# A six-layer cross network: moving small copies between engines and the fifth layer's remainder forward

## The chip, the cores and the metric

The kernel runs on one core of a Trainium2 chip. TensorE multiplies matrices into PSUM, ScalarE moves results from PSUM to SBUF and adds biases, VectorE does the elementwise arithmetic, GpSimd does small copies, and SyncE issues most of the DMAs. Each engine works through its own list of instructions in order and waits on semaphores for the others. The metric is the device time of the program in microseconds (us); lower is better. The median of the runs of the kernel before is 130.22 us (three runs, 130.12 to 130.40).

## The reference

The kernel computes a deep cross network with six layers for 4096 rows of 416 features, all in bfloat16:

```
x = x0
for l in range(6):
    x = x0 * (x @ ws[l] + bs[l]) + x
return x
```

`x0` is 4096x416, `ws` is 6x416x416, `bs` is 6x416. Every layer needs the whole previous `x`, but only of the same row.

## The kernel before, in words

The feature dimension of 416 is cut into three main chunks of 128 and a remainder of R = 32 features. In layers 0 to 4 the data is transposed: features lie on partitions, rows of the batch along the free dimension. `XM[i]` holds the three main chunks, `XR[i]` the remainder. The batch is cut into two halves s = 0 and 1 of 2048 rows; each half is four groups g of 512 columns. Because the remainder has 32 features only, its four groups are stacked on 4 x 32 partitions.

A tile (s, m) is the output chunk m of half s. `mm_full` (L206) multiplies the three main input chunks, `mm_row` (L212) adds the remainder's contribution, and `ew_main` evicts each half h of a tile: ScalarE adds the bias and writes bfloat16 (L170, in `ew_copy`), VectorE multiplies by x0 (L180) and adds the previous x (L181; L178 is layer 0's only step). Eviction uses four double banks of PSUM in rotation (`two_banks`).

The remainder's output is computed by `mm_rem` (L218 with the corner weights `WD`, L223 with the main chunks) and evicted by `ew_rem` (ScalarE L194; VectorE L197 in layer 0, L199 and L200 later). `rem_pair` does this for both halves of one layer; its matmuls read all the main chunks of the previous layer, both halves. `WD` holds a copy of the 32x32 corner of each layer's weights, at another place for each group, taken from `WR`, the last 32 weight rows (`fill_wd`, L134). `bsb` holds the biases for the last layer, copied onto four groups of 32 partitions (L111).

The order of work is written out by hand, and the program order is each engine's order. In layers 1 to 4 the six tiles go by pairs (ta, tb) for n = 0, 2, 4: full matmuls of ta, eviction of ta, for n = 2 the layer's remainder (`rem_pair`), full matmuls of tb, its row matmuls, the first row matmuls of the next tile, eviction of tb. The fifth layer (l = 4) is the one whose output feeds the last layer (`feeds_last`).

The last layer (l = 5) is computed the other way round: rows on partitions, 8 quads of four 128-row blocks, so that the output can be stored directly (`mm_q_full` L335, `mm_q_rows` L344 for the remainder and L348 for the bias from `bsb`). It needs the fifth layer's output in rows too, as `XLrows`: `xl_dmat` (L230) issues one DMA transpose for each tile when it is evicted. The remainder goes by a DMA transpose into a scratch tile `scrR` (L313) and by a copy into the last 32 columns of `XLrows` (L314). ScalarE casts (L403, for single blocks L416), VectorE multiplies by x0 (L404, L417) and adds `XLrows` (L405, L420), SyncE stores (L407, L409, L421).

At the start, `x0` arrives by eight DMA transposes on SyncE's queue (L77) and the remainder by three loads (L82, one on ScalarE's queue). `x0_rem` turns the remainder with VectorE transposes (L162) and copies (L163, L165). `first_layer(0)` and `first_layer(1)` do layer 0 for the two halves (L244, L252; evictions also by L187, L188 and L190 in `split_first`, and L271).

Of the kernel before, what the change touches and what calls it, by code (L numbers as in the profile page):

```python
# [16 lines left out]
def kernel(  # L17
# [7 lines left out]
    nc = tc.nc  # L25
    B, D = x0.shape
    L = ws.shape[0]
    P = 128
    NK = 3
    R = D - NK * P  # L30
    assert R == 32 and B == 4096 and D == 416 and L >= 2
    NS = 2
    NG = 4
# [20 lines left out]
    WR = const.tile([P, L, D], BF16)  # L54
    WD = const.tile([P, L, NG, R], BF16)
    bsb = const.tile([P, D], BF16)
# [4 lines left out]
    XLrows = big.tile([P, NBT, D], BF16)  # L61
    scrR = [big.tile([P, 4, P], BF16, name=f"scrR{s}") for s in range(NS)]
# [6 lines left out]
    def col0(s, g):  # L69
        return SW * s + CW * g  # L70
# [37 lines left out]
        nc.gpsimd.tensor_copy(bR[32 * g:32 * g + 32, :], bT[:, 4 * NK, 0:L])  # L108
    nc.gpsimd.tensor_scalar(out=bR[:, 0:1], in0=bR[:, 0:1], scalar1=1.0, scalar2=None, op0=ALU.add)
    for g in range(1, NG):  # L110
        nc.gpsimd.tensor_copy(bsb[32 * g:32 * g + 32, :], bsb[0:R, :])  # L111
    for g in range(1, NG):
        nc.vector.tensor_copy(WR[32 * g:32 * g + 32, 0, :], WR[0:32, 0, :])
        nc.scalar.copy(WR[32 * g:32 * g + 32, 1, :], WR[0:32, 1, :])
    load_x0t(0, 1)
# [13 lines left out]
    for q in range(8):  # L129
        nc.sync.dma_start(X0rows[:, 4 * q:4 * q + 4, :], x0_v[:, 4 * q:4 * q + 4, :])  # L130

    def fill_wd(l0, l1):
        for g in range(NG):
            nc.gpsimd.tensor_copy(WD[32 * g:32 * g + 32, l0:l1, g, :], WR[32 * g:32 * g + 32, l0:l1, NK * P:D])  # L134

    fill_wd(0, 1)

    PS = psum.tile([P, 8, CW], FP32)

# [3 lines left out]
    def two_banks():  # L143
        n = turn[0]
        i = first_order[n] if n < len(first_order) else (2, 1, 0, 3)[(n - len(first_order)) % 4]
        turn[0] += 1
        return PS[:, 2 * i:2 * i + 2, :]
# [10 lines left out]
    def x0_rem(s, p0, p1, parts):  # L158
        XRv = XR[0][p0:p1, CW * s:CW * s + CW].rearrange("p (j t) -> p j t", t=16)
        n = 16 // len(parts)  # L160
        for a, copy in enumerate(parts):
            nc.vector.transpose(out=xrt[s][p0:p1, n * a:n * a + n, :], in_=xrem[s][p0:p1, n * a:n * a + n, :])  # L162
            copy(XRv[:, :, n * a:n * a + n], xrt[s][p0:p1, n * a:n * a + n, :].rearrange("p t j -> p j t"))  # L163
        for a in range(p0, p1, 64):
            nc.vector.tensor_copy(XRx[s][64 - a:128 - a, :], XR[0][a:a + 64, CW * s:CW * s + CW])  # L165
# [71 lines left out]
    def first_layer(s):  # L237
        cur, nxt = XM[0], XM[1]

        def full(pt, m, h, gl, first, last):  # L240
            c0 = col0(s, 2 * h + gl)
            for k in range(NK):
                for q0, q1 in [(32 * q, 32 * q + 32) for q in range(4)] if s == 1 and h == 1 else ((0, P),):
                    nc.tensor.matmul(pt[q0:q1, gl, :], lhsT=WM[:, 0, k, 128 * m + q0:128 * m + q1], rhs=cur[:, k, c0:c0 + CW],  # L244
                                     start=(first and k == 0), stop=(last and k == NK - 1),
                                     tile_position=(0, q0) if s == 1 and h == 1 else None, skip_group_check=True)

        def row(pt, m, h, swapped, first):
            for gl in range(2):
                r0 = 32 * ((2 * h + gl + 2 * swapped) % 4)  # L250
                src = XRx[s][r0:r0 + 32, :] if swapped else XR[0][r0:r0 + 32, CW * s:CW * s + CW]
                nc.tensor.matmul(pt[:, gl, :], lhsT=WR[r0:r0 + 32, 0, 128 * m:128 * m + 128], rhs=src,  # L252
                                 start=first, stop=(not first), tile_position=(r0, 0), skip_group_check=True)

        pa = [two_banks() for m in range(NK)]
        for m, gl in ((0, 0), (1, 0), (2, 0), (0, 1), (1, 1), (2, 1)) if s == 0 else ((0, 0), (1, 0), (0, 1), (1, 1), (2, 0), (2, 1)):
            full(pa[m], m, 0, gl, True, False)
        pb = [two_banks()]
        row(pa[0], 0, 0, 0, False)
        if s == 1:  # L260
            row(pb[0], 0, 1, 0, True)
        row(pa[2], 2, 0, 0, False)
        row(pa[1], 1, 0, 1, False)
        if s == 0:
            closing = [split_first(s, 0, 0, pa[0], nxt)]
            closing.append(split_first(s, 2, 0, pa[2], nxt))
            t1 = ew_copy(0, 1, pa[1])
            for close in closing:
                close()
            x0_rem(0, 64, 128, (nc.scalar.copy, nc.vector.tensor_copy))  # L270
            nc.vector.tensor_tensor(out=nxt[:, 1, 0:2 * CW], in0=t1, in1=XM[0][:, 1, 0:2 * CW], op=ALU.mult)  # L271
            pb += [two_banks() for m in range(1, NK)]
            for m, gl in ((0, 0), (1, 0), (2, 0), (0, 1), (1, 1), (2, 1)):
                full(pb[m], m, 1, gl, True, False)
            row(pb[0], 0, 1, 0, False)
            row(pb[1], 1, 1, 0, False)
            row(pb[2], 2, 1, 1, False)
            split_first(s, 0, 1, pb[0], nxt)()
            x0_rem(1, 0, 128, (nc.vector.tensor_copy,))
            for m in range(1, NK):  # L280
                ew_main(0, s, m, 1, pb[m], cur, nxt)
            return None
        split_first(s, 0, 0, pa[0], nxt)()
        for m in (2, 1):
            ew_main(0, s, m, 0, pa[m], cur, nxt)
        full(pb[0], 0, 1, 0, False, False)
        rem_first(0)
        pb += [two_banks() for m in range(1, NK)]
        full(pb[1], 1, 1, 0, True, False)
        full(pb[0], 0, 1, 1, False, True)  # L290
        ew_main(0, s, 0, 1, pb[0], cur, nxt)
        full(pb[1], 1, 1, 1, True, False)
        for gl in range(2):
            full(pb[2], 2, 1, gl, True, False)
        row(pb[1], 1, 1, 0, False)
        row(pb[2], 2, 1, 1, False)
        pt = new_pts()
        mm_row(1, 0, 0, pt, XR[1], True, False)
        for m in range(1, NK):
            ew_main(0, s, m, 1, pb[m], cur, nxt)  # L300
        return pt
# [4 lines left out]
    def rem_pair(l, cur, curR, nxtR, feeds_last):  # L306
        pr2 = two_banks()
        for s in range(NS):
            mm_rem(l, s, pr2[:, s, :], cur, curR)
        for s in range(NS):  # L310
            ew_rem(l, s, pr2[:, s, :], curR, nxtR)
            if feeds_last:
                nc.sync.dma_start_transpose(out=scrR[s][:], in_=nxtR[:, CW * s:CW * s + CW])  # L313
                nc.gpsimd.tensor_copy(XLrows[:, 16 * s:16 * s + 16, NK * P:D].rearrange("p (g i) r -> p i g r", g=NG),  # L314
                                      scrR[s][:].rearrange("p i (g r) -> p i g r", g=NG))

    def rem_first(s):
        pr = two_banks()
        mm_rem(0, s, pr[:, 0, :], XM[0], XR[0])
        ew_rem(0, s, pr[:, 0, :], XR[0], XR[1])  # L320
# [29 lines left out]
                                 skip_group_check=True)  # L350

    first_layer(0)
    fill_wd(1, L)
    opened = first_layer(1)


    for l in range(1, LL):
        cur, curR = XM[1 + (l - 1) % 2], XR[1 + (l - 1) % 2]
        nxt, nxtR = XM[1 + l % 2], XR[1 + l % 2]
        feeds_last = (l == LL - 1)  # L360
        tiles = [(s, m) for s in range(NS) for m in range(NK)]
        pts = {tiles[0]: opened}

        def close(t):
            s, m = t
            for h in range(2):
                ew_main(l, s, m, h, pts[t][h], cur, nxt)
            if feeds_last:
                xl_dmat(s, m, nxt)

        for n in range(0, len(tiles), 2):
            ta, tb = tiles[n], tiles[n + 1]
            for g in range(NG):
                mm_full(l, ta[0], ta[1], g, pts[ta], cur, False, True)
            close(ta)
            if n == 0 and l == 1:
                rem_first(1)
            if n == 2:
                rem_pair(l, cur, curR, nxtR, feeds_last)
            pts[tb] = new_pts()  # L380
            for g in range(NG):
                mm_full(l, tb[0], tb[1], g, pts[tb], cur, True, False)
            mm_row(l, tb[0], tb[1], pts[tb], curR, False, True)
            opened = new_pts()
            if n + 2 < len(tiles):
                tc_ = tiles[n + 2]
                mm_row(l, tc_[0], tc_[1], opened, curR, True, False)
                pts[tc_] = opened
            elif not feeds_last:
                mm_row(l + 1, 0, 0, opened, nxtR, True, False)  # L390
            else:
                mm_q_rows((0,), (opened,), None)
            close(tb)

    o4 = [big.tile([P, NG, D], BF16, name=f"o4_{q}") for q in range(3)]

# [89 lines left out]
```

## Time and profile before

| what | value |
|---|---|
| median of the runs | 130.22 us |
| the profiled execution | 130.57 us, of which the span 128.8 us |
| TensorE busy | 122.7 us, 95% |
| VectorE busy | 105.2 us, 82% |
| ScalarE busy | 85.0 us, 66% |
| GpSimd busy | 9.2 us, 7% |
| granted TensorE clock | 0.999 |

The span runs from the first to the last instruction; some 1.8 us of the profiled execution lie around it. A line of the profile names the start and the length in us, the engine, the source line, the operation, the tile written and those read, the shapes, the number of instructions merged, and in brackets how long the engine was idle before and what ended that. A row with "q" behind the engine is a DMA issue on that engine's queue. A busy TensorE is not TensorE at its peak, since matmuls are pipelined and their ends are modelled.

### The profile page before, as it was taken

How to read it: one execution, taken by the hardware profiler on the slowest of the kernel's cores; microseconds unless marked ns; L12 is line 12 of the kernel's file. 1: busy time of each engine (PE TensorE's matmuls, PEld its weight loads, DVE VectorE, ACT ScalarE, POOL GpSimd, SP SyncE). 2: the span in 40 equal slices, each digit the busy share in tenths (PEclk: the TensorE clock that was granted, in tenths of full speed). 3: DMA queues.
4: the chain of work that ended last, by engine and by line, in shares of the span. 5: the costliest groups of instructions: out<-in, count | busy, mean ns of one | idle time of the engine just before them, and what ended most of it. 6: DMA issues, size and time to landing. Idle time of an engine off the chain costs nothing. (4 is left out here: it accounts for less than half of the span.)

```text
span 128.8 us, 4039 instructions
## 1 busy us (share of the span) xinstructions
PE 122.7 (95%) x1731; PEld 55.2 (43%) x1731; DVE 105.2 (82%) x192; ACT 85.0 (66%) x97; POOL 9.2 (7%) x29
## 2 busy tenths in 40 slices
PE   6999999999999999999999999999999999999960
PEld 3334344454454444444444544443444454554420
DVE  3347759648597989898989898989898999999991
ACT  2357558594976674966684966684966686676860
POOL 4282000040000000000000000000000050000000
PEclk9999999999999999999999999999999999999999
DMA  3999999999991000000000000000699989998563
GB/s 95 267 155 193 195 157 242 217 321 336 333 329 47 0 3 5 0 5 0 5 0 5 0 0 5 0 5 0 46 204 190 128 163 211 87 332 267 180 226 103
DMA packets 41933, 16.28 MB, mean 126 GB/s; under 512 B 30838, under 2 KB 41916, under 8 KB 41916
## 3 DMA queue, kind: packets, MB, share of 16 engines
q1 hardware_dynamic: 40384, 15.59, 56.4%
q10 hardware_dynamic: 1532, 0.44, 1.7%
q8 instruction: 13, 0.21, 0.7%
q14 instruction: 4, 0.03, 0.1%
HBM read 6.07 MB, written 3.41 MB: 74 GB/s over the span
## 5 line engine op out<-in xcount | busy, mean ns | idle before, releaser
L170 ACT ACTIVATE t<-PS,bM 128x1024 bf16<-128x1024 f32 x56 | 58.1, 1114 | 24.2 <-PE PS L212 22.8
L206 PE MATMUL PS<-XM,WM 128*32 128x512 bf16 x1152 | 65.2, 379 | 0.0
L206 PEld LDWEIGHTS <-WM 128*32 128x32 bf16 x1152 | 29.7, 97 | 33.8 <-issue 5.1
L180 DVE TENSOR_TENSOR t<-t,XM 128x1024 bf16<-128x1024 bf16 x48 | 33.3, 694 | 5.3 <-ACT t L170 5.3
L181 DVE TENSOR_TENSOR XM<-t,XM 128x1024 bf16<-128x1024 bf16 x48 | 33.7, 702 | 2.9
L335 PE MATMUL PS<-WM,XM 128*128 128x416 bf16 x96 | 17.9, 340 | 0.0
L244 PE MATMUL PS<-XM,WM 128*32 128x512 bf16 (+1 forms) x126 | 16.4, 379 | 0.2 <-DMA XM<-in_x_dram 0.2
L403 ACT CAST t<-PS 128x832 bf16<-128x832 f32 x12 | 10.1, 854 | 4.2 <-PE PS L335 3.1
L335 PEld LDWEIGHTS <-XM 128*128 128x128 bf16 x96 | 8.9, 98 | 8.6 <-issue 2.1
L244 PEld LDWEIGHTS <-WM 128*32 128x32 bf16 (+1 forms) x126 | 7.3, 97 | 8.6 <-issue 1.4
L223 PE MATMUL PS<-XM,WM 128*32 128x512 bf16 x120 | 8.2, 379 | 0.0
L405 DVE TENSOR_TENSOR o<-t,XLrows 128x832 bf16<-128x832 bf16 x12 | 7.1, 592 | 0.5
L212 PE MATMUL PS<-XR,WR 32*128 32x512 bf16 x96 | 7.5, 379 | 0.0
L314 POOL COPY XLrows<-scrR 128x512 bf16<-128x512 bf16 x2 | 1.6, 838 | 75.8 <-DMA scrR<-XR 75.8
L404 DVE TENSOR_TENSOR t<-t,X0rows 128x832 bf16<-128x832 bf16 x12 | 7.0, 585 | 0.0
L194 ACT ACTIVATE t<-PS,bR 128x512 bf16<-128x512 f32 x10 | 6.8, 696 | 0.0
L178 DVE TENSOR_TENSOR XM<-t,XM 128x1024 bf16<-128x1024 bf16 x7 | 4.7, 689 | 2.6 <-ACT t L170 2.5
L151 PE MATMUL PS<-warm 128*128 128x512 bf16 (+2 forms) x13 | 4.6, 536 | 1.0 <-DVE warm L87 1.0
L162 DVE STREAM_TRANSPOSE xrt<-xrem 64x256 bf16<-64x256 bf16 (+1 forms) x5 | 2.2, 476 | 4.0 <-DMA xrem<-in_x_dram 4.0
L187 ACT ACTIVATE t<-PS,bM 128x512 bf16<-128x512 f32 x4 | 2.6, 685 | 3.5 <-PE PS L252 3.5
L416 ACT CAST t<-PS 128x416 bf16<-128x416 f32 x8 | 4.0, 505 | 1.0 <-PE PS L335 0.8
L223 PEld LDWEIGHTS <-WM 128*32 128x32 bf16 x120 | 3.3, 97 | 3.2
(45 smaller groups left out, 55.6 us busy)
## 6 DMA issues: line engine op xcount, KB each, us to landing
X0rows<-in_x_dram SPq DMA_DIRECT2D x8, 416.0 KB, 7.8
WM<-in_ws_dram SPq DMA_DIRECT2D x5, 312.0 KB, 6.0
out_dram<-o SPq DMA_DIRECT2D x3, 416.0 KB, 4.0
out_dram<-o SPq DMA_DIRECT2D x6, 208.0 KB, 2.1
out_dram<-o SPq DMA_DIRECT2D x8, 104.0 KB, 1.7
WR<-in_ws_dram SPq DMA_DIRECT2D x4, 104.0 KB, 5.7
WM<-in_ws_dram ACTq DMA_DIRECT2D x1, 312.0 KB, 3.3
XM<-in_x_dram SPq DMA_TRANSPOSE x8, 4.8
```

The costliest lines, as they stand in the source:

```text
L170: nc.scalar.activation(t[:], pt.rearrange("p a b -> p (a b)"), ACT.Identity, bias=bM[:, m, l:l + 1], scale=1.0)
L180: nc.vector.tensor_tensor(out=t, in0=t, in1=x0c, op=ALU.mult)
L181: nc.vector.tensor_tensor(out=nxt[:, m, c0:c0 + 2 * CW], in0=t, in1=cur[:, m, c0:c0 + 2 * CW], op=ALU.add)
L194: nc.scalar.activation(tr[:, 0:CW], pr, ACT.Identity, bias=bR[:, l:l + 1], scale=1.0)
L206: nc.tensor.matmul(pts[g // 2][32 * q:32 * q + 32, g % 2, :], lhsT=WM[:, l, k, 128 * m + 32 * q:128 * m + 32 * q + 32], rhs=cur[:, k, c0:c ...
L212: nc.tensor.matmul(pts[g // 2][:, g % 2, :], lhsT=WR[32 * g:32 * g + 32, l, 128 * m:128 * m + 128], rhs=curR[32 * g:32 * g + 32, CW * s:CW ...
L223: nc.tensor.matmul(pr[32 * g:32 * g + 32, :], lhsT=WM[:, l, k, NK * P:D], rhs=cur[:, k, c0:c0 + CW], start=False, stop=(k == NK - 1), tile ...
L244: nc.tensor.matmul(pt[q0:q1, gl, :], lhsT=WM[:, 0, k, 128 * m + q0:128 * m + q1], rhs=cur[:, k, c0:c0 + CW], start=(first and k == 0), sto ...
L335: nc.tensor.matmul(py[g // 2][:, g % 2, 0:D], lhsT=xL[:, k, q_cols(q, g)], rhs=WM[:, LL, k, :], start=(first and k == 0), stop=((not first ...
L403: nc.scalar.copy(tv, py[h][:, :, 0:D])
L404: nc.vector.tensor_tensor(out=tv, in0=tv, in1=X0rows[:, b0:b0 + 5:4, :], op=ALU.mult)
L405: nc.vector.tensor_tensor(out=o, in0=tv, in1=XLrows[:, b0:b0 + 5:4, :], op=ALU.add)
```

## The change

Four things move:

- GpSimd's three copies of `bsb` go from the beginning to behind GpSimd's filling of the corner weights of layers 1 to 5, between the first layer's two halves.
- The four copies that fill layer 0's corner weights go from GpSimd to VectorE, into the first layer's first half, behind the first group's closing multiplications and ahead of the second part of `x0_rem`.
- The two copies of the remainder into `XLrows` go from GpSimd to ScalarE, and from right behind each transpose to behind the eviction of tile (1,0).
- In the fifth layer `rem_pair` comes behind the first tile (0,0) instead of the third (0,2), with its matmuls, evictions and the two transposes into `scrR`.

```diff
     for g in range(1, NG):
-        nc.gpsimd.tensor_copy(bsb[32 * g:32 * g + 32, :], bsb[0:R, :])
-    for g in range(1, NG):
         nc.vector.tensor_copy(WR[32 * g:32 * g + 32, 0, :], WR[0:32, 0, :])
...
-    def fill_wd(l0, l1):
+    def fill_wd(eng, l0, l1):
         for g in range(NG):
-            nc.gpsimd.tensor_copy(WD[32 * g:32 * g + 32, l0:l1, g, :], WR[32 * g:32 * g + 32, l0:l1, NK * P:D])
-
-    fill_wd(0, 1)
+            eng.tensor_copy(WD[32 * g:32 * g + 32, l0:l1, g, :], WR[32 * g:32 * g + 32, l0:l1, NK * P:D])
...
             for close in closing:
                 close()
+            fill_wd(nc.vector, 0, 1)
             x0_rem(0, 64, 128, (nc.scalar.copy, nc.vector.tensor_copy))
...
                 nc.sync.dma_start_transpose(out=scrR[s][:], in_=nxtR[:, CW * s:CW * s + CW])
-                nc.gpsimd.tensor_copy(XLrows[:, 16 * s:16 * s + 16, NK * P:D].rearrange("p (g i) r -> p i g r", g=NG),
-                                      scrR[s][:].rearrange("p i (g r) -> p i g r", g=NG))
+
+
+    def xl_rem():
+        for s in range(NS):
+            nc.scalar.copy(XLrows[:, 16 * s:16 * s + 16, NK * P:D].rearrange("p (g i) r -> p i g r", g=NG),
+                           scrR[s][:].rearrange("p i (g r) -> p i g r", g=NG))
...
     first_layer(0)
-    fill_wd(1, L)
+    fill_wd(nc.gpsimd, 1, L)
+    for g in range(1, NG):
+        nc.gpsimd.tensor_copy(bsb[32 * g:32 * g + 32, :], bsb[0:R, :])
     opened = first_layer(1)
...
-            if n == 2:
+            if n == (0 if feeds_last else 2):
                 rem_pair(l, cur, curR, nxtR, feeds_last)
...
             close(tb)
+            if feeds_last and n == 2:
+                xl_rem()
```

## The prediction

> **What bounds the kernel now.** The profiled execution took 130.57 us, a span of 128.8 and 1.77 around it; the median of the runs shown is 130.22, 0.35 less. I work out a difference within the span and take it off the median. I read the busy shares first, then the waits, then the order of time at the start, around 88 us and at the end.
>
> ```profile
> PE 122.7 (95%) x1731; PEld 55.2 (43%) x1731; DVE 105.2 (82%) x192; ACT 85.0 (66%) x97; POOL 9.2 (7%) x29
> ```
>
> TensorE is busy 95% of the span. Its few real waits lie in the first 21 us:
>
> ```profile
> 9.81 0.61 PE L252 MATMUL PS<-XR,WR 32*128 32x512 bf16 x4
> 14.68 0.60 PE L252 MATMUL PS<-XR,WR 32*128 32x512 bf16 x4 [0.19 <-DVE XR L163]
> 20.33 0.83 PE L244 MATMUL PS<-XM,WM 128*32 128x512 bf16 x12 [0.20 <-DMA XM<-in_x_dram]
> ```
>
> The first stands 0.53 us behind the matmul before it, where such a step elsewhere takes 0.31: 0.22 us lost. The third waits for an input transpose. From 20.33 to about 124.3 TensorE has no wait that another engine ends. Behind it VectorE works without a gap that matters from 98.75 to its last addition, and the chain that ended last is VectorE's alone. GpSimd shows inside that stretch:
>
> ```profile
> 103.45 1.62 POOL L314 COPY XLrows<-scrR 128x512 bf16<-128x512 bf16 x2 [75.80 <-DMA scrR<-XR]
> ...
> 102.74 0.69 DVE L180 TENSOR_TENSOR t<-t,XM 128x1024 bf16<-128x1024 bf16 x1
> 103.46 1.15 DVE L181 TENSOR_TENSOR XM<-t,XM 128x1024 bf16<-128x1024 bf16 x1
> 104.58 1.03 DVE L180 TENSOR_TENSOR t<-t,XM 128x1024 bf16<-128x1024 bf16 x1
> 105.65 0.69 DVE L181 TENSOR_TENSOR XM<-t,XM 128x1024 bf16<-128x1024 bf16 x1
> ```
>
> While the two GpSimd copies run, two VectorE instructions take 1.15 and 1.03 us instead of 0.69.
>
> **The change, part by part.**
>
> *The remainder's columns by ScalarE.* GpSimd's two copies leave the tail. The two slowed instructions fall back to 0.69, but the second, of tile (1,2), can't start before ScalarE's eviction ends at 103.44 + 1.11 = 104.55. So VectorE would start L404 not at 107.59 but about 0.4 earlier (0.35 of the second instruction, 0.03 of waiting). The first L405 also pays: it starts 0.68 after its L404, where others take 0.62, and the one at 117.35 the same; 0.06 each, for a list of semaphores with GpSimd's in it at the first. I count the first as gained.
>
> What it adds: two ScalarE copies of 128x512 behind tile (1,0)'s evictions, ahead of those of (1,1).
>
> ```profile
> 97.60 4.13 ACT L170 ACTIVATE t<-PS,bM 128x1024 bf16<-128x1024 f32 x4 [2.21 <-PE PS L212]
> 103.44 2.12 ACT L170 ACTIVATE t<-PS,bM 128x1024 bf16<-128x1024 f32 x2 [1.71 <-PE PS L212]
> 122.74 2.09 ACT L416 CAST t<-PS 128x416 bf16<-128x416 f32 x4 [0.59 <-PE PS L335]
> ```
>
> Queued behind them are two evictions, then a pause of 1.71 us. The price of one copy is not in the trace. The nearest low end is L416 and L114, ScalarE over 416 elements a partition in 0.51 and 0.54 us; L403 takes 0.85 for 832, so 0.83 ns an element, and 512 make 0.59 to 0.62. The high end is ScalarE's L163, 0.62 us for 256 elements read 64 bytes apart: doubled, 1.24. I take 0.61, since the new copy reads its rows in order and writes runs of 32 elements, and the same access pattern cost GpSimd 0.61 in the copy that VectorE did not hold up. ScalarE's neighbours in a row overlap by about 0.1 (4 of 1.11 in 4.13), so two copies are 1.0 to 1.25 us. Eviction (1,1) then starts at 99.6 + 1.0 to 1.25, ends at 101.7 to 102.0, and its second half at 102.7 to 103.0. VectorE, at 101.41 on that tile now, waits 0.3 to 0.6; two tiles at 1.33 a half bring it to (1,2) at 104.4 to 104.7, against the eviction at 104.55. It starts L404 between 107.2 and 107.4: still 0.2 to 0.35 early. TensorE wants those two banks for the rows of the last layer at 103.23 and finds them free by at least 0.2.
>
> [...]
>
> *How much of it reaches the end.*
>
> ```profile
> 117.91 0.85 ACT L403 CAST t<-PS 128x832 bf16<-128x832 f32 x1 [0.77 <-PE PS L335]
> 118.97 0.85 ACT L403 CAST t<-PS 128x832 bf16<-128x832 f32 x1 [0.20 <-PE PS L335]
> 118.99 0.58 DVE L404 TENSOR_TENSOR t<-t,X0rows 128x832 bf16<-128x832 bf16 x1
> 125.08 0.37 DVE L417 TENSOR_TENSOR t<-t,X0rows 128x416 bf16<-128x416 bf16 x1
> ```
>
> ScalarE's casts follow TensorE, which doesn't move. VectorE trails them by 1.3 us at L404's first and by less later: the cast that begins at 117.91 ends at 118.76 and VectorE takes it at 118.99. With 0.03 for the hand-over it can be earlier there by 0.19 at most. The last cast ends at 122.74 + 2.09 = 124.83, and its L417 starts at 125.08, so the end can come 0.21 earlier at most. A lead of 0.26 to 0.4 is therefore cut to 0.18: **gain 0.18 us**, and were the lead twice that, no more than 0.21.
>
> *The fifth layer's remainder behind tile (0,0)* (layer index 4). Its 32 matmuls, two evictions, four VectorE instructions and two transposes go past tiles (0,1) and (0,2), whose work comes 1.72 us later (L218 at 92.75 to the next L206 at 94.47). At (1,0) all is as before: VectorE has two idle stretches (0.29 at 91.18 and 0.22 at 98.75) that move about. The new wait: TensorE reads there the last tile of the layer before, whose last half VectorE writes at 87.41 + 0.69 = 88.10. Tile (0,0) starts at 84.31; now the remainder begins 2.60 behind such a start (90.15 to 92.75), and its matmuls on that half come 1.51 later (two groups into the second L223): 88.42. Slack 0.26 with the hand-over; cost 0. Without that cover every tenth late would be a tenth on TensorE, with all of its queue behind it.
>
> ```profile
> 87.41 0.69 DVE L181 TENSOR_TENSOR XM<-t,XM 128x1024 bf16<-128x1024 bf16 x1
> 90.92 2.90 SPq L230 DMA_TRANSPOSE XLrows<-XM  x1
> 98.77 3.75 SPq L313 DMA_TRANSPOSE scrR<-XR  x2
> ```
>
> On SP's queue the two L313 go past two L230: they are issued at about 93.9 and 95.8 and land 3.1 later by their row, so by 98.9, before ScalarE reaches its copy at 99.6 (GpSimd waited 4.6 from the first's issue to its start; that would be 100.4 for the second and 0.15 us of waiting). The L230 of (0,1) and (0,2) go from 97.6 and 99.4; with the longest landing of their row, 6.7, the data is there at 106.1, before L405 at about 108. Those of the second half are issued as now, when VectorE has written.
>
> *First corner weights by VectorE.* Four copies of 32x32 between L190, done at 12.39, and the transposes at 13.44: VectorE idles 1.05 there for a DMA. Bounds: 0.06 each by the smallest VectorE row (L93), 0.29 by L113 (32x416 with its step), so 0.24 to 1.16. Near the small end, I take 0.7 at most: cost 0. At 1.16 the wait at 14.68 would grow by 0.11, and the one at 20.33 would take that back.
>
> *GpSimd's bias copies later.* Three of 0.53 us leave 7.78 to 9.44. VectorE's L163 there took 0.49, its twin at 14.25 took 0.37, so the matmul at 9.81 can come 0.12 earlier. But the wait at 14.68 hangs on a DMA that lands at 13.42 and the one at 20.33 on one at 20.29, neither behind GpSimd: the 0.12 is swallowed, gain 0. The copies now run at about 27.7 to 29.4 beside L178 and L180; three of them can hold VectorE for 1.6 us, and it idles 0.31, 0.31 and 1.61 there up to 33.5; TensorE reads what L178 writes there from about 35 on. Cost 0. The copied rows are read first at 103.4.
>
> Sum: 0.18 + 0 + 0 + 0. 130.22 - 0.18 = **130.04 us** (the profiled kind of execution 130.39), a change of 0.14%. A measurement of this kernel can tell some 0.2%, 0.26 us, from no change, so this reads as none.
>
> **Rivals.**
>
> 1. *The input stream gives back more.* If the transposes behind 20.33 land 0.12 earlier than in this execution (their rows spread from 4.4 to 5.9), the early matmul's 0.12 stays, and TensorE's whole line comes forward: 0.12 + 0.18 = 0.30, 129.92 us. For it: both waits end on DMA. Against it: nothing in the change starts those DMAs sooner.
>
> 2. *ScalarE's copies are long and turn the pause into a queue.* At 1.24 each, 2.26 for the pair: (1,1)'s second half is evicted at 104.0 instead of 101.7, TensorE waits 0.8 at 103.23, VectorE starts L404 0.75 later; less what the first L405 saves, 130.22 + 0.65 = 130.87. It decides from about 0.75 a copy, where the banks come free too late and eat the 0.18. For it: L163. Against it: L114 and L416.
>
> 3. *The remainder waits for layer index 3.* If VectorE is 0.7 us later at 88.10 than now, TensorE stalls 0.44, and 130.22 + 0.44 - 0.18 = 130.48. Against it: the tiles there are tied to ScalarE's evictions, which wait for TensorE (1.7 us idle).
>
> 4. *The remainder's transposes land late.* The L230 of 96.89 landed 5.8 after its issue; so late, the second copy would start at 101.6, (1,1) be evicted by 104.2, TensorE wait 1.0: 131.0. For it: DMA engines are nearly full from 93 us. Against it: only one transpose stands ahead of these two.
>
> **How the numbers follow.** Forecast 0.46, its own range 129.96 to 130.3. Rival 1 with all that ends faster 0.30. Slower 0.24: rival 2 0.10, rival 3 0.06, rival 4 0.08. The range 129.8 to 130.6 takes rival 1 in, the forecast, rival 3 and half of rival 2's prices (0.9 to 1.0 a copy), and leaves some 0.2 out. Faster by over 0.2% 0.30, within 0.46, slower 0.24.
>
> **What the profile after would show.** L181's longest falls from 1.15 to 0.69 and no GpSimd row stands behind 30 us. ScalarE has two copies of 128x512 near 99.6, 0.6 each, and VectorE an idle of 0.3 to 0.6 before (1,1). L218 of the fifth layer starts near 86.9 without a wait before 88.4. TensorE's waits at 14.68 and 20.33 stand, the one at 9.81 is 0.12 shorter. L335 starts at 103.69 as now. VectorE's last addition comes 0.18 earlier, tied to the last cast by 0.03 to 0.1. Wrong would be a wait of TensorE at 88 or 103, a ScalarE copy above 0.75, or a first layer that ends earlier than now.

## The result and the profile after

The changed kernel takes 130.71 us (median of nine runs, 130.38 to 130.87) against 130.22 (nine runs, 129.89 to 130.48): a ratio of 1.0031, 95% interval 1.0017 to 1.0045. It is slower by 0.3%, where 0.14% faster was forecast. Later runs of the same two programs put the ratio at 1.0017 (1.0005 to 1.003), so the size is nearer 0.2%. The profiled execution after took 130.72 us, its span 128.9; the one before 130.57 and 128.8, which was slower than any of before's nine timed runs. That turned out to matter.

Nearly every step that was forecast is there. Here are rows picked from the timeline of the changed kernel (start and length in us); rows between them are left out, also where no "..." stands. Its line numbers differ by a few: L132 answers to L134, L166 to L170, L176 and L177 to L180 and L181, L208 to L212, L214 to L218, L240 to L244, L310 and L315 to L313 and L314, L336 to L335, L408 and L409 to L403 and L404, L422 and L425 to L417 and L420.

```profile
12.91 0.70 DVE L132 COPY WD<-WR 32x32 bf16<-32x32 bf16 x4
...
20.14 0.83 PE L240 MATMUL PS<-XM,WM 128*32 128x512 bf16 x12
...
86.87 0.39 PE L214 MATMUL PS<-XR,WD 128*32 128x512 bf16 x4
...
93.92 2.52 SPq L310 DMA_TRANSPOSE scrR<-XR  x2
...
99.56 1.14 ACT L315 COPY XLrows<-scrR 128x512 bf16<-128x512 bf16 x2
100.59 2.13 ACT L166 ACTIVATE t<-PS,bM 128x1024 bf16<-128x1024 f32 x2
101.75 0.69 DVE L176 TENSOR_TENSOR t<-t,XM 128x1024 bf16<-128x1024 bf16 x1 [0.30 <-ACT t L166]
103.64 3.34 PE L336 MATMUL PS<-WM,XM 128*128 128x416 bf16 x18
104.54 0.69 DVE L176 TENSOR_TENSOR t<-t,XM 128x1024 bf16<-128x1024 bf16 x1
107.20 0.58 DVE L409 TENSOR_TENSOR t<-t,X0rows 128x832 bf16<-128x832 bf16 x1
118.75 0.59 DVE L409 TENSOR_TENSOR t<-t,X0rows 128x832 bf16<-128x832 bf16 x1 [0.19 <-ACT t L408]
125.15 0.65 DVE L425 TENSOR_TENSOR o<-t,XLrows 128x416 bf16<-128x416 bf16 x2
```

No GpSimd row stands behind 30 us. The fifth layer's remainder begins at 86.87 without a wait. Its transposes are issued at 93.9, ahead of ScalarE's copies at 99.56, and these take 1.14 together (0.62 each). VectorE waits 0.30 for the eviction behind them. Its first multiplication of the last layer starts at 107.20 instead of 107.59, from 118.75 on it is tied to ScalarE's casts, and its last addition ends at 125.81 instead of 126.02: 0.21 earlier. TensorE's last layer starts at 103.64, 0.05 earlier than before. Up to VectorE's end the forecast gain is there.

It is lost behind that, in work that nobody touched. The last stores, of the kernel before (L421) and then of the one after (L426): the view of the tile `out_dram` from 124.6 us on, durations of the issue in ns, and the time from issue to landing:

```profile
L421 SPq DMA_DIRECT2D out_dram<-o x4: 332/332/369, 124.3 to 126.2; - x4
DMA to landing us min/median/max: 1.7/1.7/1.7
```

```profile
L426 SPq DMA_DIRECT2D out_dram<-o x3: 332/333/728, 125.0 to 126.0; - x3
DMA to landing us min/median/max: 2.1/2.2/2.4
```

The same stores of 104 KB land 0.4 to 0.7 later after their issue, and the last of them takes 0.728 us to issue instead of 0.369. The DMA queues between 124.5 and 126.9 us, before and then after (packets, MB, share of the 16 DMA engines):

```profile
q1 hardware_dynamic: 573, 0.43, 53.4%
```

```profile
q1 hardware_dynamic: 556, 0.41, 51.2%
q14 instruction: 1, 0.01, 1.9%
```

One packet on queue 14, of kind "instruction", is new among the stores. The trace gives it 8192 bytes and a start at 125.84 us; 1.9% of 16 engines over 2.4 us are 0.73 us on one engine. That it is a piece of an engine's program is the author's reading of that kind; which engine's list it moves with is measured below. Another packet of this size on this queue comes in every profile 0.1 to 0.4 us behind the last data of the stores (127.66 in before, 127.85 in after). It is not the one that moves, though the expectation for before again takes it for that one, and it is not counted below. The last store landed at 127.91 before and at 128.11 after: 0.21 earlier by VectorE, 0.41 later by its landing.

### The profile page after: what moved, and what is told of

It reads as the page before. It is cut to its first block, busy times and chain, and to the rows that moved or that the text cites. A ratio compares the mean times of both kernels' runs of the same rounds, so it can differ in the third digit from the quotient of the medians.

```text
span 128.9 us, 4033 instructions
## 1 busy us (share of the span) xinstructions
PE 123.1 (95%) x1730; PEld 55.0 (43%) x1731; DVE 105.3 (82%) x196; ACT 86.0 (67%) x99; POOL 7.2 (6%) x23
## 3 DMA queue, kind: packets, MB, share of 16 engines
HBM read 6.07 MB, written 3.41 MB: 74 GB/s over the span
## 4 chain that ended last, share of the span: by engine, by line
PE 87%; DVE 5%; DMA 4%; ACT 1%; issue 1%; DVEq 0%
PE PS L202 49%; PE PS L240 13%; PE PS L336 9%; PE PS L208 5%; PE PS L219 5%; DMA XM<-in_x_dram 4%; PE PS L214 2%; DVE o L425 2%; PE PS L248 2%; DVE t L422 1%; PE PS L345 1%; DVE o L410 1%; DVE t L409 1%; PE PS L349 1%; ACT t L408 1%
## 5 line engine op out<-in xcount | busy, mean ns | idle before, releaser
L166 ACT ACTIVATE t<-PS,bM 128x1024 bf16<-128x1024 f32 x56 | 58.2, 1114 | 22.9 <-PE PS L208 21.8
L176 DVE TENSOR_TENSOR t<-t,XM 128x1024 bf16<-128x1024 bf16 x48 | 32.9, 686 | 5.7 <-ACT t L166 5.7
L177 DVE TENSOR_TENSOR XM<-t,XM 128x1024 bf16<-128x1024 bf16 x48 | 33.4, 696 | 2.6
L336 PE MATMUL PS<-WM,XM 128*128 128x416 bf16 x96 | 17.9, 340 | 0.0
L240 PE MATMUL PS<-XM,WM 128*32 128x512 bf16 (+1 forms) x125 | 17.2, 386 | 0.1
L408 ACT CAST t<-PS 128x832 bf16<-128x832 f32 x12 | 10.1, 854 | 4.2 <-PE PS L336 2.7
L336 PEld LDWEIGHTS <-XM 128*128 128x128 bf16 x96 | 8.9, 98 | 8.6 <-issue 2.1
L240 PEld LDWEIGHTS <-WM 128*32 128x32 bf16 (+1 forms) x126 | 7.3, 99 | 9.5 <-issue 3.0
L208 PE MATMUL PS<-XR,WR 32*128 32x512 bf16 x96 | 7.5, 379 | 0.0
L409 DVE TENSOR_TENSOR t<-t,X0rows 128x832 bf16<-128x832 bf16 x12 | 7.0, 584 | 0.2 <-ACT t L408 0.2
L421 ACT CAST t<-PS 128x416 bf16<-128x416 f32 x8 | 4.0, 505 | 1.0 <-PE PS L336 0.8
L184 DVE SCALAR_TENSOR_TENSOR XM<-PS,bM,XM 128x512 bf16<-128x512 f32 x4 | 2.9, 746 | 1.2 <-PE PS L248 1.2
```

Source lines behind the costliest of these rows:

```text
L166: nc.scalar.activation(t[:], pt.rearrange("p a b -> p (a b)"), ACT.Identity, bias=bM[:, m, l:l + 1], scale=1.0)
L176: nc.vector.tensor_tensor(out=t, in0=t, in1=x0c, op=ALU.mult)
L177: nc.vector.tensor_tensor(out=nxt[:, m, c0:c0 + 2 * CW], in0=t, in1=cur[:, m, c0:c0 + 2 * CW], op=ALU.add)
L208: nc.tensor.matmul(pts[g // 2][:, g % 2, :], lhsT=WR[32 * g:32 * g + 32, l, 128 * m:128 * m + 128], rhs=curR[32 * g:32 * g + 32, CW * s:CW ...
L336: nc.tensor.matmul(py[g // 2][:, g % 2, 0:D], lhsT=xL[:, k, q_cols(q, g)], rhs=WM[:, LL, k, :], start=(first and k == 0), stop=((not first ...
L408: nc.scalar.copy(tv, py[h][:, :, 0:D])
```

## The experiments

Two questions were open: which half of the change costs the time, and whether the late stores are the cost or a sign of something else. The theory that formed from the traces: such a transfer follows a fixed entry of ScalarE's instruction list, and the two added copies move it from behind the end to among the last stores. Rivals: TensorE gets through layer 0 later ("front" in the expectations, where the theory of the transfer is called "end" and later "page"); the time comes from the earlier remainder or from ScalarE's copies themselves (with the earlier transposes, "ports" in the expectations); it is GpSimd's shorter list that moves the transfer; the stores meet `XLrows`' last transposes.

**Both kernels again, and each half alone.** The first two are the programs before and after, unchanged. The third has the tail part (remainder forward, copies by ScalarE) and the start as before; the fourth the start part (corner weights by VectorE, bias copies later) and the tail as before. Against the changed kernel, the edit of the third and of the fourth:

```diff
     for g in range(1, NG):
+        nc.gpsimd.tensor_copy(bsb[32 * g:32 * g + 32, :], bsb[0:R, :])
+    for g in range(1, NG):
...
+    fill_wd(nc.gpsimd, 0, 1)
...
-            fill_wd(nc.vector, 0, 1)
...
     fill_wd(nc.gpsimd, 1, L)
-    for g in range(1, NG):
-        nc.gpsimd.tensor_copy(bsb[32 * g:32 * g + 32, :], bsb[0:R, :])
```

```diff
-    def xl_rem():
-        for s in range(NS):
-            nc.scalar.copy(XLrows[:, 16 * s:16 * s + 16, NK * P:D].rearrange("p (g i) r -> p i g r", g=NG),
-                           scrR[s][:].rearrange("p i (g r) -> p i g r", g=NG))
+                nc.gpsimd.tensor_copy(XLrows[:, 16 * s:16 * s + 16, NK * P:D].rearrange("p (g i) r -> p i g r", g=NG),
+                                      scrR[s][:].rearrange("p i (g r) -> p i g r", g=NG))
...
-            if n == (0 if feeds_last else 2):
+            if n == 2:
...
-            if feeds_last and n == 2:
-                xl_rem()
```

> The kernel before, unchanged, as a control. In the two profiles so far VectorE's last addition ends at 126.02 before and 125.81 after, 0.21 earlier as forecast, yet the last store lands at 127.91 before and 128.11 after. Two theories for the loss of 0.49 us in the medians. 'End': an 8192-byte instruction transfer at 125.84, among the last stores of the kernel after, holds three of them up by 0.4 to 0.7 each; before, the transfer starts at 127.66, behind the last row of output. 'Front': TensorE gets through layer 0 later; the profiled execution of before (130.57) was slower than each of its nine timed runs (129.89 to 130.48), so its front may not be the usual one. Here both expect a ratio of 1.000 within 0.0015. End: no 8192-byte transfer between 124.5 and 127.0, last store 1.6 to 1.75 us from issue to landing. Front: the first matmul behind the last input transpose, at 20.33 in the first profile, comes 0.2 to 0.5 earlier in this one.

> The kernel after, unchanged, as a control. Both theories expect a ratio of 1.0031 within 0.0015. End: again an 8192-byte transfer within the last stores, between 125.5 and 126.2, and the last two stores at 2.1 us or more from issue to landing. Front: no such thing need be there; layer 0's last half starts 0.2 to 0.5 later than in the usual execution of before.

> The tail's two parts alone: the remainder's columns by ScalarE, the fifth layer's remainder behind tile (0,0); the beginning is as before. By the forecast's own sum 130.22 - 0.18 = 130.04, ratio 0.9986. End, if the tail's parts bring the transfer forward: VectorE's last addition 0.2 earlier than before but ratio 1.002 to 1.004. Front: the forecast's gain stays, ratio 0.998 to 0.9995, and VectorE's last addition near 125.8.

> The beginning's two parts alone: the corner weights' four copies by VectorE, GpSimd's bias copies behind layer 0's first half; the tail is as before, GpSimd's two copies in it too. Forecast: no change, ratio 1.000. Front: the whole loss and the missing gain are here, ratio 1.003 to 1.006. End: ratio 1.000 if the tail's parts move the transfer, 1.003 if these do (GpSimd's or VectorE's number of instructions).

Measured, with twelve runs each and 35 of the kernel before (130.26 us):

| run | us | ratio, 95% | queue-14 packet among the last stores | issue to landing of the last three stores |
|---|---|---|---|---|
| before again | 130.14 | 0.9992 (0.9978 to 1.0006) | none | 1.66, 1.67, 1.78 |
| after again | 130.52 | 1.0017 (1.0005 to 1.003) | 125.97, 0.69 us | 2.31, 2.15, 2.06 |
| tail part only | 130.56 | 1.002 (1.001 to 1.003) | 125.86, 0.76 us | 2.49, 2.25, 2.13 |
| start part only | 130.17 | 0.9992 (0.9979 to 1.0005) | none | 1.66, 1.67, 1.80 |

The loss is all in the tail part, and it comes with the packet. The start part is worth nothing that can be measured. The front theory had its sign in before again: the first matmul behind the last input transpose stands there at 19.75 us instead of 20.33. But that time moves from execution to execution in both kernels: over all twelve profiles of this document it is 19.75 to 20.33 with the old start (seven profiles, mean 20.09) and 19.86 to 20.33 with the new one (five, mean 20.03).

Before, run again, also showed what the forecast gain was worth: its last addition ended 1.02 us behind ScalarE's last cast, as in after, not 1.19 as in the execution that the prediction was made from. GpSimd's two copies stood elsewhere against VectorE. The timelines of this run:

```profile
102.70 1.69 POOL L314 COPY XLrows<-scrR 128x512 bf16<-128x512 bf16 x2 [76.72 <-DMA scrR<-XR]
```

```profile
102.22 0.68 DVE L180 TENSOR_TENSOR t<-t,XM 128x1024 bf16<-128x1024 bf16 x1
102.94 0.98 DVE L181 TENSOR_TENSOR XM<-t,XM 128x1024 bf16<-128x1024 bf16 x1
104.06 0.87 DVE L180 TENSOR_TENSOR t<-t,XM 128x1024 bf16<-128x1024 bf16 x1
106.90 0.58 DVE L404 TENSOR_TENSOR t<-t,X0rows 128x832 bf16<-128x832 bf16 x1
```

GpSimd starts 0.24 ahead of VectorE's L181 instead of 0.01, the two slowed instructions take 0.98 and 0.87 instead of 1.15 and 1.03, and the last layer begins early enough that the casts set the end.

**Is it ScalarE's list, whatever is in it?** Four kernels move the list alone. Counted with its waits, the trace of before has 192 entries on ScalarE, that of after 194. The first edit takes after back to 192, by giving two of ScalarE's weight copies at the start to VectorE. The second adds two copies of one column to before near 4 us, where ScalarE is idle. The third adds three small memsets to GpSimd in the kernel with the tail part only, so that its list is as long as before's (48 entries); the diff shows this against the tail part alone, without the line that allots `spare`. The fourth adds eighteen one-column copies to after, in ScalarE's pauses in layers 1 to 3; their results are used by nothing.

```diff
-        nc.scalar.copy(WR[32 * g:32 * g + 32, 1, :], WR[0:32, 1, :])
+        (nc.scalar.copy if g == 1 else nc.vector.tensor_copy)(WR[32 * g:32 * g + 32, 1, :], WR[0:32, 1, :])
```

```diff
     nc.scalar.activation(dz[:, 1:2], dz[:, 0:1], ACT.Identity, bias=dz[:, 0:1], scale=1.0)
+    for _ in range(2):
+        nc.scalar.copy(dz[:, 1:2], dz[:, 0:1])
```

```diff
     fill_wd(nc.gpsimd, 1, L)
+    for _ in range(3):
+        nc.gpsimd.memset(spare[:], 0.0)
```

```diff
             close(tb)
+            if n == 0 and not feeds_last:
+                for _ in range(6):
+                    nc.scalar.copy(dz[:, 1:2], dz[:, 0:1])
```

> The kernel after, with two of ScalarE's three early copies of layer 1's remainder weights given to VectorE, so that ScalarE's list is as long as before (two fewer than after). Theory 'page': the 8192-byte transfer is ScalarE's next piece of program; after's two added copies let ScalarE reach the end of a piece right at its last instruction (transfer 1.05 after its last cast in three profiles), before it reached it only behind the kernel. Then this one has no 8192-byte transfer between 124.5 and 126.8, stores that land in 1.65 to 1.8, and the forecast's gain: ratio 0.9986, 0.997 to 0.9995. Rival 'GpSimd': GpSimd's shorter list or its early end moves the transfer; then it stays near 125.9 and the ratio at 1.002 to 1.003. Rival 'ports': ScalarE's copies or the earlier transposes themselves slow the last stores; ratio 1.002 to 1.003 without the transfer.

> The kernel before, with two ScalarE copies of one column more, in its idle time near 4 us; nothing else is changed. Page: the transfer comes at 125.5 to 126.2, about 1.05 behind ScalarE's last cast, the last three stores land in 2.1 to 2.5 instead of 1.7, ratio 1.003 to 1.004 (the delay of 0.4 us without the tail's gain). GpSimd and ports: ratio 1.000, transfer near 127 to 127.7.

> The tail's parts alone, and three tiny GpSimd fills of a spare tile behind 27 us, so that GpSimd's list is as long as before. GpSimd: the transfer goes back behind 127, ratio 0.9986. Page and ports: nothing changes against the tail's parts alone, transfer at 125.8 to 126, ratio 1.002 within 0.0015.

> The kernel after, with 18 ScalarE copies of one column more, six in each of three idle stretches of ScalarE in layers 1 to 3. Page: ScalarE reaches the end of its piece 18 list entries earlier, some nine casts before its end, so the transfer comes at 118.5 to 120.5; the stores of that time are late, those of the end are not (1.65 to 1.8), ratio 0.9986, 0.997 to 1.000. GpSimd and ports: transfer at 125.9 or none, ratio 1.002 to 1.003.

Measured, with twelve runs each and 35 of the kernel before (130.24 us):

| run | us | ratio, 95% | queue-14 packet among the last stores | issue to landing of the last three stores |
|---|---|---|---|---|
| after, list as before | 130.14 | 0.9987 (0.9974 to 1.0001) | none | 1.65, 1.66, 1.79 |
| before, two more | 130.51 | 1.002 (1.0005 to 1.0034) | 125.78, 0.78 us | 2.47, 2.22, 2.09 |
| tail part, GpSimd's list as before | 130.46 | 1.0018 (1.0007 to 1.0028) | 125.63, 0.76 us | 2.49, 2.25, 2.11 |
| after, eighteen more | 130.07 | 0.9987 (0.9975 to 0.9999) | none (118.65, 0.31 us) | 1.66, 1.67, 1.82 |

The second is the decisive one: the kernel before, with two copies of a single column 100 us ahead of the end, gets all of the loss. Its ratio is below the 1.003 to 1.004 that was expected, but the interval still excludes no change. Its view of `out_dram` from 124.3 us, then its queues between 125.5 and 126.8, and last the view of `out_dram` of after with the list as before, whose queues have no instruction row in that stretch:

```profile
L423 SPq DMA_DIRECT2D out_dram<-o x4: 332/332/767, 124.1 to 125.9; - x4
DMA to landing us min/median/max: 1.7/2.2/2.5
```

```profile
q14 instruction: 1, 0.01, 3.7%
```

```profile
L426 SPq DMA_DIRECT2D out_dram<-o x3: 332/332/369, 124.8 to 125.8; - x3
DMA to landing us min/median/max: 1.7/1.7/1.8
```

GpSimd's list has nothing to do with it, and neither have the copies themselves, the remainder's place or the transposes: the kernel with eighteen more has all of the change, and its last stores land as fast as before's. Its packet comes at 118.65 and takes 0.31, 7 us ahead of the last store. There an expectation missed: the stores of that time were to be late, but those issued at 117.08, 118.21 and 119.61 land in 2.09, 2.07 and 2.04 us, and the same stores take 2.03 to 2.25 in the other profiles. The packet fell into a pause between the data of two stores. The busy share of the 16 DMA engines between 118 and 119.5 us, in 40 slices of 0.0375 us, is below a tenth from 118.68 to 119.09:

```profile
DMA  6899999999999987470000000000045999989998
```

**How sharp is the place?** One added copy, and six, in the same line as the two above, with one run of each beside one of before (130.58 us).

> The kernel before with one tiny ScalarE copy near 4 us instead of two: one look, for the edge. In the ten traces so far the 8192-byte transfer follows ScalarE's 191st list entry; with two more that entry is its last before the closing barrier, with one more it would be the barrier's first entry, behind the last store's landing. Page: no such transfer between 124.5 and 126.8, the last store in 1.7 to 1.85, TensorE's last matmul to the end of the span 4.65 to 4.85. If it is not one entry that decides, but ScalarE's early extra work, the transfer is at 125.5 to 126.2 and that stretch is 4.95 to 5.1.

> The same with six. Page: the 191st entry is four earlier than with two, two casts before ScalarE's end; the transfer comes at about 124.0 to 125.2, the stores issued from 123.5 to 124.5 are the late ones, the last one lands in 1.7 to 2.0, and from TensorE's last matmul to the end of the span it is 4.7 to 4.95, between the two cases.

One more took 130.74, six more 130.40. With one more no packet falls among the stores; it comes at 129.27, and the last stores land in 1.66, 1.66 and 1.75 us. With six more it comes at 124.18 and takes 0.59; two earlier stores, issued at 123.57 and 124.13, land in 2.21 and 1.98, and the last three in 1.66, 1.66 and 1.78, so the end pays nothing. In ordinary words, from the records of ScalarE's list (the entry's end, and the start of the 8192-byte packet behind it; a drain is the record's DRAIN, a wait its EVENT_SEMAPHORE, and the closing barrier is the group of these behind the last store):

```
kernel             entries   191st entry                      packet starts
before               192     drain of the closing barrier     128.33 -> 129.34
before, one more     193     wait of the closing barrier      128.26 -> 129.27
after                194     drain behind the last cast       124.83 -> 125.84
before, two more     194     drain behind the last cast       124.76 -> 125.78
before, six more     198     wait ahead of the last but one   123.20 -> 124.18
after, 18 more       212     wait among the pairs' casts      117.50 -> 118.65
```

In the profiles of before, after and all ten runs this packet follows the end of the 191st entry by 1.0 to 1.3 us, and where the entry moves it moves with it. In after, where the two copies stand behind it, an earlier such packet (46.74 us, behind the 63rd entry) keeps its place; in before with two more, where they stand ahead of it, it moves from 46.78 to 43.78. This earlier place is less sharp. Where the 63rd entry is a wait (seven profiles) the packet comes 1.01 to 1.03 behind its end, but where it is an activation (five) the packet comes before that activation has ended; in all twelve it comes 1.01 to 1.06 behind the start of the 62nd. So the distance of 128 entries between the two places is good to about one entry; 8192 bytes by 128 make 64 bytes an entry, an estimate from these two places alone. Among the last stores the packet's cost was not hidden: it is 0.30 us at the end of the span (worked out below).

Another expectation missed. With one more, the end of the span came 5.135 us behind the start of the last matmul, where 4.65 to 4.85 was expected, though its stores were fast. That is some 0.4 more than in the profiles without the packet among their stores (4.72, below). The larger part stands in its VectorE rows (the timelines of GpSimd and VectorE of that run):

```profile
103.34 1.72 POOL L316 COPY XLrows<-scrR 128x512 bf16<-128x512 bf16 x2 [77.23 <-DMA scrR<-XR]
```

```profile
103.34 0.69 DVE L183 TENSOR_TENSOR XM<-t,XM 128x1024 bf16<-128x1024 bf16 x1
104.46 1.14 DVE L182 TENSOR_TENSOR t<-t,XM 128x1024 bf16<-128x1024 bf16 x1 [0.43 <-ACT t L172]
```

Here GpSimd and VectorE started within 0.001 us of each other. VectorE took its 0.69, and GpSimd's first copy 1.16 instead of 0.61. VectorE then had to wait for the eviction and was held up itself, 1.14 for 0.69, on the instruction that nothing covers. The lag of its last addition behind the last cast was 1.295 instead of 1.02. A further 0.18 lies behind the last landing, from which it is 1.03 us to the end of the span, against 0.83 to 0.85 in the other profiles: ScalarE's drain in the closing barrier, the entry right behind the 191st, starts 0.36 behind the wait ahead of it, where before's starts 0.07 behind. The cause of this part stays open.

The held-up VectorE is the cost that the change was forecast to remove, and it depends on a tenth of a microsecond. When the first GpSimd copy started 0.24 to 0.33 ahead of VectorE's instruction (three profiles), the lag was 1.02; with 0.13 it was 1.08, with 0.01 it was 1.19, and with 0.001 it was 1.295. In the six profiles with GpSimd's copies in the tail each of the eleven VectorE instructions that were held up ends 0.54 to 0.55 us behind the end of a GpSimd copy, and a held-up copy 0.47 behind the end of a VectorE instruction. The order of the starts agrees where it can be told: GpSimd's first copy was 0.01 ahead in before and 0.24 in before again, and VectorE's instructions were held up (1.15 and 1.03; 0.98 and 0.87, for 0.69). In the run with one more VectorE's instruction at 103.34 took its 0.69 and the copy was held up, but the record's starts are too close to tell. What the two engines meet at is not shown here.

## Why the prediction was wrong

- **Corner weights and bias copies: right.** Both were costed at nothing; the start part alone measures 0.9992 (0.9979 to 1.0005). The four copies took 0.70, the figure that was taken, inside VectorE's idle time. The three bias copies at 26.97 held VectorE up once (0.90 for 0.69) without a wait of TensorE. The waits at 14.68 and 20.33, which were to stand, are not in the profile after, because TensorE's full clock came 1.5 us later in that execution (at 7.14 instead of 5.64, below) and it reached the data late; layer 0 ended level all the same.
- **The fifth layer's remainder: right.** No wait at 88 us, and the transposes landed at 96.38 and 97.66, before the copies. Rivals 3 and 4 did not occur.
- **The price of ScalarE's copy: right.** 0.62, the pair 1.14, against 0.61 and 1.0 to 1.25. VectorE waited 0.30 (0.3 to 0.6 forecast), started the last layer at 107.20 (107.2 to 107.4), and TensorE did not wait at 103. Rival 2 did not occur.
- **"Gain 0.18 us": right for the execution that was read (0.21), mis-sized for the kernel.** The lag of the last addition behind the last cast, with GpSimd's copies in the tail, was 1.19, 1.02, 1.02, 1.02, 1.295 and 1.08 (before, before again, start part only, and before with two, one and six more); without them 1.02 in all profiles. The mean excess is 0.17 + 0 + 0 + 0 + 0.28 + 0.06 over 6, 0.08 us. The hint was in the prediction's first paragraph: the profiled execution was 0.35 us slower than the median, and a cost that was larger in it than in most was taken off the median.
- **The sum: here the step failed.** "0.18 + 0 + 0 + 0" prices work added to ScalarE by its time alone and lets the stores behind VectorE's last addition stay as they are. The missing term is the transfer on queue 14. Its size: from the start of the last matmul to the end of the span the five kernels that have the packet among the last stores take 5.04, 4.98, 5.05, 5.01 and 5.05 us (mean 5.03), the four that have neither it nor a longer lag 4.705, 4.73, 4.72 and 4.74 (mean 4.72): 0.30 us. Less the 0.08 of gain, this is +0.22, or 0.17%, beside 1.0017, 1.002 and 1.0018 measured for after again and the two kernels with the tail part, and at the lower end of the first interval, 1.0017 to 1.0045; the 1.0031 of the first measurement did not come again. Before with two more has the transfer without the gain: 0.30 would be 1.0023, measured 1.002. None of the four rivals held it. What is left of the first measurement's 0.49 us beyond this 0.22 is not explained.

The changed kernel without the transfer among its stores took 130.07 and 130.14 us, against 130.24 for before; the interval of the one with eighteen idle copies (0.9975 to 0.9999) only just excludes no change. Whether the change by itself is a gain of about 0.1 us stays open: before, run against itself in the other comparison, read 0.9992.

## What to carry to other kernels

Two instructions more on ScalarE moved an 8 KiB packet of kind "instruction" here from 129.34 us, behind the last stores, to 125.84 (after) and 125.78 (before with two more), among their data, and the last three landed in 2.06 to 2.49 us instead of 1.65 to 1.82. So compare the "instruction" rows of the DMA queues over the last few microseconds whenever the end grows behind work that nobody touched. Here a few instructions more or fewer on that engine moved it: two fewer or eighteen more cleared the end of the kernel after, while two more on the kernel before brought the transfer in and six more took it past, to where the end paid nothing. And a cost read from one execution that lies off the median should be looked up in a second execution before it is counted as a gain.

## What the hardware showed that was not expected

- One 8 KiB transfer of kind "instruction", 0.69 to 0.78 us long, held up three stores of 104 KB by 0.3 to 0.8 us each (2.06 to 2.49 from issue to landing instead of 1.65 to 1.82), and doubled the issue of the last one (from 0.37 us to between 0.71 and 0.77). The same transfer at 118.65, in a pause between stores, took 0.31 us and held up none.
- Two instructions of one column at 4 us cost 0.26 us at 126 us (0.2% of 130.24).
- The time at which TensorE's full clock is granted differs by execution: from 5.64 us in the profile before, 7.14 in after, 3.78 in before again, 6.60 in after again. It stayed for 122.88 us in ten of the twelve profiles and for 119.466 in two. The difference is 3.414, and the two are 36 and 35 times that within 0.03; a grant that changes in steps of about 3.41 us is the author's estimate from these two lengths alone. Until 7.14 after's first matmuls came every 427 ns instead of 216, the closing row matmuls of the first group stood at 10.39 instead of 9.81, and at 20.14 TensorE was no longer behind: before had waited 0.19 us ahead of 14.68 and 0.20, for a DMA, ahead of 20.33. Whether part of the spread of 0.6 us between runs of one kernel comes from this stays open: the three earliest grants (3.78 to 4.09) have the first matmul behind the last input transpose at 19.75 to 19.91, but those at 5.25 and 6.97 have it at 19.89 too, and the one at 4.49 at 20.24.
